# Polysketch attention and a multiplicative FFN: a planner with measured durations, key sums in four operations, filled waits and new ranks

## The chip, the cores and the metric

The kernel runs on one core of a Trainium2 chip. The metric is the device time of one execution in microseconds (us); lower is better. The profiled execution gives every instruction's start and duration on the core's engines: TensorE (PE, with its weight loads as PEld), VectorE (DVE), ScalarE (ACT), GpSimd (POOL) and SyncE (SP, which issues the DMAs).

## The reference

```python
def phi(x):                                   # S1, S2: 8 x 32; x: 4 x 4 x 1088 x 32
    a = np.einsum('rd,bhsd->bhsr', S1, x)
    b = np.einsum('rd,bhsd->bhsr', S2, x)
    return np.einsum('bhsi,bhsj->bhsij', a, b).reshape(*x.shape[:-1], r * r)
q_p, k_p = (phi(q), phi(k))
kv = np.einsum('bhsf,bhsd->bhfd', k_p, v)     # key sums
z = np.sum(k_p, axis=2)
num = np.einsum('bhsf,bhfd->bhsd', q_p, kv)
den = np.einsum('bhsf,bhf->bhs', q_p, z)[..., None] + 1e-06
x = (num / den).transpose(0, 2, 1, 3).reshape(4352, 128)
out = ((x @ w1) * (x @ w2) @ w3) @ w_out      # w1, w2: 128 x 1024; w3: 1024 x 1024; w_out: 1024 x 128
```

S1, S2 and the four FFN weights come in as float64 and reach the kernel as raw words; q, k and v are float32.

## The kernel before

**Key side, once for each of the 4 batches.** VectorE forms the maximum of the keys (`peak`), a rounded leading part and the remainder (`first`, `second`, `kk`). TensorE sums products over the keys into one PSUM tile, `ps_kvz`, in `products` (L688): `gs` is the Gram part from `kk`, `kv` the sum of key features `kp` times v. Each is a run of very small products, 32 columns wide: for a batch 64 products in each half of the Gram part (`gs0`, `gs1`), 24 for the 64 keys beyond 1024 (`rg`), 32 in each half of `kv` and 8 for the rest (`rv`). In TensorE's instructions each product is one product record and one weight load; the counts of a batch are 152 for `gs` and 72 for `kv`. The features `kp` come from the keys by head: `tr` (VectorE transposes, L618), `ab` (TensorE, L624), `ab_t` (L635), `kp` (L608). From the sums VectorE and TensorE then make the small matrices that the queries need: `fin1`, `T_mm`, `T_pair`, `N_mm`, `N_pair`, `kz` (L745 to L785).

**Query side, for 8 groups of 512 queries' positions in all heads and a rest (group 8).** Transposes (L1009), `grid`, `lead` (ScalarE), `rem`, then `ay` (TensorE), `split`, `dens`, `dens2` and `phi` (VectorE, L969, tile `ph`), `phT` (TensorE, L976, tile `ps_ph`), `pT` (ScalarE copy), `nd` (TensorE, L993, tile `ps_x`) and a ScalarE copy to `xT` (L1000), the FFN's input.

**FFN, for each group and 8 chunks of 128 hidden columns.** `a` (L1090) and `b` (L1100) on TensorE, the copy of `a` on ScalarE (L1095), `mul` on VectorE (L1105, tile `ab`), `o` (L1111, tile `ps_o`) on TensorE, and a transpose `oT` (VectorE, L1116) that is stored. w3 and w_out are folded into one matrix `w3o` (`ps_wt` L522, `ps_w3o` L534). The weights come in 22 chunks; ScalarE reads their words in three operations (L375, L378, L339) and VectorE makes float32 of them in two (`join` L387, `add` L390).

**The order.** The first 34 us are a list written by hand (L1165), with products of zeros (`idle`, L322) in TensorE's waits. All else is given as operations to a planner, `Plan` (L43 to L137): name, engine, duration, what is read and written, and a rank. It keeps a clock for each engine, and of the operations that can start within 0.1 us of the earliest it takes the one of lowest rank:

```python
t0 = min(c)[0] + 0.1
t, r, i = min((x for x in c if x[0] <= t0), key=lambda x: (x[1], x[2]))
```

PSUM has one bank each for `out`, `ps_kvz`, `t`, `wa` and `wb` and three (`h`) that `a` and `b` share. What the planner gives is issued in that order, and each engine keeps it (L1204 to L1211), so the planner's durations decide only the order; a wait on the chip is whatever the real durations make of it.

Of the kernel before, what the change touches and what calls it, by code (L numbers as in the profile page):

```python
# [37 lines left out]
COLUMNS = {"ay": 32, "ab": 32, "gs": 32, "kv": 32, "nd": 64}  # L38
TURN = 0.1
LATENCY = {"PE": 0.27, "DVE": 0.2, "ACT": 0.23, "POOL": 0.3, "SP": 2.5}  # L40


class Plan:  # L43
# [36 lines left out]
    def order(self):  # L80
# [3 lines left out]
        columns = 128  # L84
        turn = {}
# [14 lines left out]
        while left:  # L100
            best = {}
            for i in left:
# [38 lines left out]
def kernel(  # L141
# [178 lines left out]
    def idle(times, n=256):  # L320
        for _ in range(times):
            nc.tensor.matmul(idle_ps[:, :n], zeros[:, :128], zeros[:, :n], start=True, stop=True)  # L322
    idle(24)
    sgn = [consts.tile([128, CW], I32, tag=f"sgn{i}", name=f"sgn{i}") for i in range(2)]
# [190 lines left out]
    def weight_ops(first):  # L515
# [23 lines left out]
        for n in range(first, len(chunks)):  # L539
# [15 lines left out]
            for us, f in zip((0.62, 0.62, 0.7), words):  # L555
                p.op("words", "ACT", us, f, (("raw", n),), (("cv", n),), 0.3 if w_in else 3)
            for us, f in ((0.65, join), (0.62, add)):
                p.op("conv", "DVE", us, f, (("cv", n),), dst, 0.5 if w_in else 1.5)
            if name == "w3":
                ko, half = divmod(i, NH)  # L560
                p.op("w3_t", "PE", 0.44, lambda i=i: w3_t(i), dst, (("wa", "t", i),), 1)
                p.op("w3_t_copy", "ACT", 0.57, lambda i=i: w3_t_copy(i), (("wa", "t", i),), (("w3T", ko),), 1)
                if half == NH - 1:
                    p.op("w3_mm", "PE", 1.75, lambda ko=ko: w3_mm(ko), (("w3T", ko), *(("wo", x) for x in range(NC * DM // CW))),
                         (("wb", "mm", ko),), 1)
# [106 lines left out]
    def rest_ops(m, behind):  # L672
        nat, tr, tr_copy, ab, b_copy, feat = rest_steps(m)
        p.op("r_tr", "PE", 0.15, lambda: run_all((nat, tr)), (("k", 2 * m),), (("t", "r_tr"),), 0, (behind,))
        p.op("r_tr_copy", "ACT", 0.2, tr_copy, (("t", "r_tr"),), (("kT", "r"),), 0.5)
        p.op("r_ab", "PE", 0.22, ab, (("kT", "r"),), (("t", "r_ab"),))
# [3 lines left out]
    def k_steps(b):  # L680
# [561 lines left out]
```

## Time and profile before

| | us |
|---|---|
| runs: median (lowest to highest) of 3 | 305.8 (304.82 to 306.84) |
| profiled execution, its own time | 304.33 |
| its span, first to last instruction | 302.6 |
| TensorE busy | 279.8 |
| VectorE busy | 204.4 |
| ScalarE busy | 127.3 |
| mean granted TensorE clock | 0.989 |

The profiled execution is 1.5 us shorter than the median run, and 1.73 us of its time lie outside the span. Names in the profile's rows are those of tiles, an arrow from right to left reads "is made from", and the bracket at the end of a row is the idle time of that engine just before it with what ended it. A row of the timeline begins with its start in us.

### The profile page before, as it was taken

The page shows a single profiled execution, that of the slowest core. Times are in us where ns is not written, and L with a number is a line of the kernel's source. Part 1 is how long each engine was busy: PE and PEld are TensorE (multiplying, and loading weights), DVE is VectorE, ACT ScalarE, POOL GpSimd, SP SyncE. Part 2 cuts the span into 40 slices and gives each one's busy share as a digit, 9 for nine tenths or more (in the row PEclk, how much of TensorE's full clock was granted, in tenths as well). Part 3 has the DMA queues.
Part 4 walks back from the last instruction along what each step waited for, and adds up shares of the span by engine and source line. Part 5 has one row for each costly group of instructions (what it writes and reads, how often), then busy time and mean ns, then how long its engine had stood idle before and what let it go on. Part 6 is the DMA issues. An engine that isn't in the chain of part 4 may idle for free.

```text
span 302.6 us, 5558 instructions
## 1 busy us (share of the span) xinstructions
PE 279.8 (92%) x2214; PEld 159.7 (53%) x2214; DVE 204.4 (68%) x505; ACT 127.3 (42%) x244; POOL 7.1 (2%) x12
## 2 busy tenths in 40 slices
PE   7987889769999898959999999999999999999984
PEld 5866335336777556436644446454444453444653
DVE  6989799958999979994481279855845583642330
ACT  4634785839778591317302231224132333232111
POOL 0000000000000010000100001001000100000000
PEclk9999999979999999997999999999999999999999
DMA  5649995357781020000022010001100100200202
GB/s 156 215 100 310 254 319 229 89 192 208 221 202 69 0 76 2 3 1 0 2 35 35 0 27 12 2 1 18 19 0 5 31 0 0 35 2 1 35 2 50
DMA packets 28729, 22.37 MB, mean 74 GB/s; under 512 B 20000, under 2 KB 25248, under 8 KB 28704
## 3 DMA queue, kind: packets, MB, share of 16 engines
q1 hardware_dynamic: 28704, 22.03, 26.1%
q8 instruction: 17, 0.28, 0.4%
q14 instruction: 8, 0.07, 0.1%
HBM read 19.80 MB, written 2.23 MB: 73 GB/s over the span
## 4 chain that ended last, share of the span: by engine, by line
PE 74%; DVE 13%; DMA 6%; issue 3%; SPq 1%; ACT 1%; DVEq 0%; ACTq 0%
PE ps_o L1111 19%; PE b_ps L1100 18%; PE a_ps L1090 17%; PE ps_kvz L688 5%; DMA k_sb<-in_k_dram 5%; PE ps_w3o L534 4%; PE ps_x L993 2%; PE ps_wt L522 2%; PE ps_ph L976 2%; PE ps_c L894 2%; DVE ab L1105 2%; DMA qh<-in_q_dram 1%; DVE ph L969 1%; DVE kk L663 1%; PE ps_ab L624 1%
## 5 line engine op out<-in xcount | busy, mean ns | idle before, releaser
L1105 DVE TENSOR_TENSOR ab<-ffa,b_ps 128x512 f32<-128x512 f32 (+1 forms) x72 | 46.9, 653 | 61.6 <-PE b_ps L1100 60.7
L1095 ACT COPY ffa<-a_ps 128x512 f32<-128x512 f32 (+1 forms) x72 | 40.4, 561 | 109.7 <-PE a_ps L1090 109.0
L1090 PE MATMUL a_ps<-xT,w 128*128 128x512 f32 (+1 forms) x144 | 71.5, 578 | 1.7 <-ACT xT L1000 1.6
L1100 PE MATMUL b_ps<-xT,w 128*128 128x512 f32 (+1 forms) x144 | 71.6, 579 | 0.8 <-DVE ab L1105 0.5
L1111 PE MATMUL ps_o<-ab,w3o 128*128 128x512 f32 (+1 forms) x144 | 68.3, 577 | 0.8 <-DVE oT L1116 0.8
L1090 PEld LDWEIGHTS a_ps<-xT,w 128*128 128x128 f32 x144 | 26.6, 192 | 31.4 <-issue 20.5
L1100 PEld LDWEIGHTS b_ps<-xT,w 128*128 128x128 f32 x144 | 26.4, 192 | 30.3 <-issue 25.4
L1111 PEld LDWEIGHTS ps_o<-ab,w3o 128*128 128x128 f32 x144 | 25.7, 190 | 23.9 <-issue 19.6
L534 PEld LDWEIGHTS ps_w3o<-wo,w3T 128*128 128x128 f32 x128 | 15.4, 192 | 5.2 <-issue 4.1
L983 ACT COPY pT<-ps_ph 128x512 f32<-128x512 f32 (+1 forms) x18 | 9.4, 567 | 19.7 <-PE ps_ph L976 19.7
L339 ACT CAST sgn<-cv_c 128x512 f16<-128x512 f32 x22 | 16.9, 770 | 0.0
L534 PE MATMUL ps_w3o<-wo,w3T 128*128 128x128 f32 x128 | 15.8, 277 | 0.3 <-DVE bs L959 0.3
L375 ACT ACTIVATE cv_c<-raw 128x512 f32<-128x512 f32 x22 | 15.0, 682 | 0.8 <-DVE wo L387 0.8
L976 PE MATMUL ps_ph<-ident,ph 128*128 128x128 f32 x68 | 10.1, 290 | 5.4 <-DVE ph L969 5.3
L378 ACT ACTIVATE cv_m<-raw 128x512 int32<-128x512 uint32 x22 | 14.9, 676 | 0.3 <-DVE w3c L390 0.3
L322 PE MATMUL idle_ps<-zeros 128*128 128x256 bf16 x88 | 12.6, 308 | 1.7 <-DVE zeros L317 1.7
L976 PEld LDWEIGHTS ps_ph<-ident,ph 128*128 128x128 f32 x68 | 8.2, 147 | 10.1 <-issue 6.5
L387 DVE SCALAR_TENSOR_TENSOR w3c<-cv_c,sgn 128x512 int32<-128x512 int32 x16 | 10.8, 677 | 3.8 <-ACT sgn L339 3.8
L529 ACT COPY w3T<-ps_wt 128x512 f32<-128x512 f32 x16 | 9.3, 584 | 7.5 <-PE ps_wt L522 7.4
L993 PE MATMUL ps_x<-pT,kz 128*64 128x512 f32 (+1 forms) x48 | 10.8, 511 | 1.0 <-DVE k_ab L635 0.5
L322 PEld LDWEIGHTS <-zeros 128*128 128x128 bf16 x88 | 9.6, 112 | 3.8 <-DVE zeros L317 1.7
L867 POOL TENSOR_TENSOR q<-qT,q 128x512 f32<-128x512 f32 x5 | 5.8, 1154 | 230.5 <-ACT q L863 230.5
(180 smaller groups left out, 329.8 us busy)
## 6 DMA issues: line engine op xcount, KB each, us to landing
raw<-in_moe_w_dram SPq DMA_DIRECT2D x20, 512.0 KB, 5.7
qh<-in_q_dram SPq DMA_DIRECT2D x4, 544.0 KB, 6.7
k_sb<-in_k_dram SPq DMA_DIRECT2D x4, 512.0 KB, 5.2
out_dram<-oT SPq DMA_DIRECT2D x32, 64.0 KB, 1.9
kh<-in_k_dram SPq DMA_DIRECT2D x12, 128.0 KB, 5.8
v_sb<-in_v_dram SPq DMA_DIRECT2D x12, 128.0 KB, 4.4
raw<-in_moe_w_out_dram SPq DMA_DIRECT2D x2, 512.0 KB, 7.8
v_sb<-in_v_dram SPq DMA_DIRECT2D x1, 512.0 KB, 5.3
```

The source lines that it names most:

```text
L322: nc.tensor.matmul(idle_ps[:, :n], zeros[:, :128], zeros[:, :n], start=True, stop=True)
L339: nc.scalar.copy(bview(t.bitcast(F16)[:, 1:], [[2, n]]), c)
L375: nc.scalar.mul(x["c"], halves(raw[n], CW)[1].bitcast(F32), 2.0 ** -112)
L534: nc.tensor.matmul(ps["mm"], w3T[ko][:, c], wo[:, c], start=(c == 0), stop=(c == NC - 1))
L688: nc.tensor.matmul(out[h * D:(h + 1) * D], lhs, rhs, start=start, stop=stop, skip_group_check=True)
L976: nc.tensor.transpose(s["ps"][:, j * 128:(j + 1) * 128], s["ph"][:, j, 2 * p:2 * p + 2].rearrange("p h i j -> p (h i j)"), ident)
L993: nc.tensor.matmul(view(ps[64 * p:64 * (p + 1)]), kz_done[t if b is None else b][:, 64 * p:64 * (p + 1)], view(s["pT"][:, p, :n]), start=T ...
L1090: nc.tensor.matmul(a_sb[g, c, "ps"][:, :n], w1[:, c * 128:(c + 1) * 128], xT[key], start=True, stop=True)
L1095: nc.scalar.copy(a_sb[g, c][:, :n], a_sb.pop((g, c, "ps"))[:, :n])
L1100: nc.tensor.matmul(ab_sb[g, c, "ps"][:, :n], w2[:, c * 128:(c + 1) * 128], xT[key], start=True, stop=True)
L1105: nc.vector.tensor_mul(ab_sb[g, c][:, :n], a_sb.pop((g, c))[:, :n], ab_sb.pop((g, c, "ps"))[:, :n])
L1111: nc.tensor.matmul(o_ps[g][:, :n], w3o[:, c], ab_sb.pop((g, c))[:, :n], start=c == 0, stop=c == NC - 1)
```

## The change

The planner's durations are set to measured ones, most by a tenth of a microsecond or less. The key sums are four operations, `gs0`, `gs1` (with `rg`), `kv0` and `kv1` (with `rv`), each with its own place; before, they were two. A new rule counts TensorE's products: an operation is put off, in the plan's time, where more than 120 products (`MOST`) would have begun in the last 2 us (4 us in the first 60). `ps_kvz` is one tile for the whole kernel. Where TensorE waits over 0.6 us in the plan, products of zeros fill the wait; they go to columns of `ps_kvz` that nothing reads. The plan has two such places, 7 products ahead of `nd` of group 1 and 11 ahead of that group's first `a`. Ranks come from a table, `FIRST`: VectorE's key work goes from 1 to 2, `mul` from 0 to 0.55, and `o` is taken earlier (at 6 waiting chunks, was 8). Lines after the change are 21 to 26 higher.

TensorE around the end of batch 1's Gram sums (`ps_kvz`), before:

```order
L688 MATMUL ps_kvz<-kkr_218 32x64
L688 MATMUL ps_kvz<-kkr_218 32x32 x2
L522 MATMUL ps_wt<-ident,w3c 128x128 x4
L1100 MATMUL b_ps<-xT,w_71 128x512
L1090 MATMUL a_ps<-xT,w_70 128x512
L624 MATMUL ps_ab<-kT,S12blk 32x256 x8
L522 MATMUL ps_wt<-ident,w3c 128x128 x4
L1100 MATMUL b_ps<-xT,w_71 128x512
```

The same place after, at the end of the first half of these sums:

```order
L710 MATMUL ps_kvz<-kk 32x64
L710 MATMUL ps_kvz<-k_sb,kk 32x32
L1121 MATMUL b_ps<-xT,w_71 128x512
L544 MATMUL ps_wt<-ident,w3c 128x128 x4
L1111 MATMUL a_ps<-xT,w_70 128x512
L646 MATMUL ps_ab<-kT,S12blk 32x256 x8
L710 MATMUL ps_kvz<-kk 32x64
L710 MATMUL ps_kvz<-k_sb,kk 32x32
```

The 152 products of the Gram part stood in one run; now 64 are followed by five other operations and then 88. In batches 2 and 3 all 224 products stood in one run behind `ay`; now 64 stand alone, and 160 follow after `ab` and a `w3o` (batch 2) or after a `b` and an `a` (batch 3).

TensorE around the transposes `ps_ph` of the fourth query group, before:

```order
L443 MATMUL ps_N<-Ts,P_437 128x8
L1100 MATMUL b_ps<-xT,w_71 128x512
L1090 MATMUL a_ps<-xT,w_70 128x512
L1100 MATMUL b_ps<-xT,w_71 128x512
L781 MATMUL ps_kz<-ident,kvm 128x128
L976 MATMUL ps_ph<-ident,ph 128x128 x8
L522 MATMUL ps_wt<-ident,w3c 128x128 x4
L993 MATMUL ps_x<-pT,kz_1281 64x512 x2
L534 MATMUL ps_w3o<-wo,w3T 128x128 x8
```

and after:

```order
L556 MATMUL ps_w3o<-wo,w3T 128x128 x8
L1121 MATMUL b_ps<-xT,w_71 128x512
L1132 MATMUL ps_o<-ab,w3o 128x512
L1111 MATMUL a_ps<-xT,w_70 128x512
L997 MATMUL ps_ph<-ident,ph 128x128 x8
L1121 MATMUL b_ps<-xT,w_71 128x512
L544 MATMUL ps_wt<-ident,w3c 128x128 x4
L1014 MATMUL ps_x<-pT,kz_1269 64x512 x2
L544 MATMUL ps_wt<-ident,w3c 128x128 x4
L1111 MATMUL a_ps<-xT,w_70 128x512
L710 MATMUL ps_kvz<-kk 32x64
```

These transposes stood behind batch 2's sums and their `ps_T`, `ps_N` and `ps_kz`; now they and `ps_x` stand ahead of all of them.

VectorE at the `ph` that these transposes read, before:

```order
L776 TENSOR_TENSOR Rh<-Na,mask4n 128x32
L776 TENSOR_TENSOR Rf<-Na,mask_96 128x32
L776 TENSOR_TENSOR Rl<-Nb,mask_96 128x32
L1105 TENSOR_TENSOR ab<-ffa,b_ps 128x512 x2
L608 TENSOR_TENSOR kp<-k_ab 128x1024
L969 TENSOR_TENSOR ph<-ay,bs 128x1024
L390 ISA w3c<-w3c,cv_m 128x1024
```

and after:

```order
L975 TENSOR_REDUCE den<-pr 128x32
L977 SCALAR_TENSOR_TENSOR rc<-den 128x16
L978 RECIPROCAL rc<-rc 128x16
L980 TENSOR_TENSOR bs<-ay_C,rc 128x128
L990 TENSOR_TENSOR ph<-ay,bs 128x1024
L1126 TENSOR_TENSOR ab<-ffa,b_ps 128x512
L412 ISA w3c<-w3c,cv_m 128x1024
```

Between `bs` (the last step of the denominator) and `ph` stood `fin1`, `T_pair` and `N_pair` of batch 2, two `kp` of batch 3 and six `mul`; now nothing stands there.

TensorE's end, before:

```order
L1100 MATMUL b_ps<-xT,w_71 128x256
L1090 MATMUL a_ps<-xT,w_70 128x256
L1111 MATMUL ps_o<-ab,w3o 128x512
L1100 MATMUL b_ps<-xT,w_71 128x256
L1111 MATMUL ps_o<-ab,w3o 128x512
L1111 MATMUL ps_o<-ab,w3o 128x256 x8
```

and after:

```order
L1111 MATMUL a_ps<-xT,w_70 128x256
L1132 MATMUL ps_o<-ab,w3o 128x512
L1121 MATMUL b_ps<-xT,w_71 128x256
L1111 MATMUL a_ps<-xT,w_70 128x256
L1121 MATMUL b_ps<-xT,w_71 128x256
L1132 MATMUL ps_o<-ab,w3o 128x256 x8
```

The last `o` of group 7 (128x512) stood right ahead of the eight of the rest (128x256), which write the same bank; now three half products stand between. The diff, with the table of durations cut to a line or two:

```diff
-COLUMNS = {"ay": 32, "ab": 32, "gs": 32, "kv": 32, "nd": 64}
+COLUMNS = {"ay": 32, "ab": 32, "gs0": 32, "gs1": 32, "kv0": 32, "kv1": 32, "nd": 64}
+PRODUCTS = {"ay": 48, "ay2": 32, "ab": 16, "gs0": 64, "gs1": 88, "kv0": 32, "kv1": 40, "w3_mm": 16, "w3_t": 4}
+MOST = 120
+FIRST = {"words": 3, "conv": 1.5, "early": 1.5, "k": 2, "KX": 6, "q": 1, "q_act": 0.5, "k_act": 1, "a": 2, "b": 1.9, "o": 1.5,
+         "many": 6, "late": 3, "w3_t": 1, "w3_t_copy": 1, "w3_mm": 1, "k1": 1, "mul": 0.55}
...
+                if engine == "PE":
+                    room = MOST - PRODUCTS.get(ops[i][0], 2)
+                    for at, count in reversed(issued):
+                        room -= count
+                        if room < 0:
+                            t = max(t, at + (4.0 if at < 60 else 2.0))
+                            break
...
-    def idle(times, n=256):
+    kvz_ps = psum.tile([128, 512], F32, tag="kvz", name="ps_kvz")
+    late_ps = kvz_ps[:, 256:]
+    def idle(times, late=False):
         for _ in range(times):
-            nc.tensor.matmul(idle_ps[:, :n], zeros[:, :128], zeros[:, :n], start=True, stop=True)
+            nc.tensor.matmul(late_ps if late else idle_ps[:, :256], zeros[:, :128], zeros, start=not late, stop=True,
+                             skip_group_check=late)
     idle(24)
+    nc.tensor.matmul(late_ps, zeros[:, :128], zeros, start=True, stop=True)
...
-                ps = psum.tile([128, 128], F32, tag="kvz", name="ps_kvz")
+                ps = kvz_ps[:, :128]
...
-        op("first", "DVE", 1.25 if even else 1.0, (("k", b), ("gk", b)), (("kk", b),), rank)
+        op("first", "DVE", 1.63 if even else 1.25, (("k", b), ("gk", b)), (("kk", b),), rank)
...
-        p.op("gs", "PE", 2.2, lambda: run_all(st[x] for x in ("gs0", "gs1", "rg")), (("k", b), ("kk", b), ("kkr", m)),
+        p.op("gs0", "PE", 0.85, st["gs0"], (("k", b), ("kk", b)), (("kvz", b),))
+        p.op("gs1", "PE", 1.1, lambda: run_all(st[x] for x in ("gs1", "rg")), (("k", b), ("kk", b), ("kkr", m)), (("kvz", b),))
+        p.op("kv0", "PE", 0.6, st["kv0"], (("kp", b, 0), ("v", b)), (("kvz", b),))
+        p.op("kv1", "PE", 0.7, lambda: run_all(st[x] for x in ("kv1", "rv")), (("kp", b, 1), ("v", b), ("kpr", m)),
              (("kvz", b),))
-        p.op("kv", "PE", 1.35, lambda: run_all(st[x] for x in ("kv0", "kv1", "rv")),
-             (("kp", b, 0), ("kp", b, 1), ("v", b), ("kpr", m)), (("kvz", b),))
...
-                 lambda tiles, end: 1.5 if pend(tiles, end) > 8 else 3)
+                 lambda tiles, end: FIRST["o"] if pend(tiles, end) > FIRST["many"] else FIRST["late"])
...
+    busy = 0.0
     for t, n in p.order():
+        if p.ops[n][1] == "PE":
+            if t - busy > 0.6:
+                idle(int((t - busy - 0.3) / 0.107), late=True)
+            busy = t + p.ops[n][2]
         p.ops[n][3]()
```

More of the change, by code (lines that the diff above doesn't have):

```diff
@@ L1027, in op @@
             if rank is None:
-                rank = {"PE": 0, "DVE": 1, "ACT": 0.5, "POOL": 0}[engine]
+                rank = {"PE": 0, "DVE": FIRST["q"], "ACT": FIRST["q_act"], "POOL": 0}[engine]
             return p.op(f"{name}", engine, us, st[name], reads, writes, rank, after)
@@ L1034, in q_ops @@
         elif not skip:
[L1035 removed]
+            op("tr", "DVE", 0.75 if half else 0.62, (("qh", b),), (qT, ("qTr", b))[:1 + half], after=begin)
             if half and b + 2 < B:
                 p.op("load", "SP", 1.7, lambda: load_by_head("q", b + 2), (), (("qh", b + 2),))
[L1038 to L1039 removed]
+        op("grid", "DVE", 0.35 + 0.6 * w, (qT,), (("gq", g),), after=begin)
+        op("lead", "ACT", 0.2 + 1.2 * w, (qT, ("gq", g)), (("q1", g), ("q2", g)))
         op("rem", "DVE" if lean else "POOL", 0.62 if lean else 1.1, (qT, ("q1", g), ("q2", g)), (("q2", g),))
@@ L1176 @@
         for b in bs:
-            p.hold((which, b), 3.0 * (b - 1))
+            p.hold((which, b), 3.0 * (b - 1) + (2.4 if which == "qh" and b == 1 else 0))
     p.hold(("xT", 0), 0.3)
```

66 lines of the change are left out of this document (32 added, 34 removed).

## The prediction

> **What bounds the kernel now.** I read the page first: the busy line, then the slices for TensorE and its granted clock.
>
> ```profile
> PE 279.8 (92%) x2214; PEld 159.7 (53%) x2214; DVE 204.4 (68%) x505; ACT 127.3 (42%) x244; POOL 7.1 (2%) x12
> ...
> PE   7987889769999898959999999999999999999984
> PEclk9999999979999999997999999999999999999999
> ...
> q8 instruction: 17, 0.28, 0.4%
> ...
> PE 74%; DVE 13%; DMA 6%; issue 3%; SPq 1%; ACT 1%; DVEq 0%; ACTq 0%
> ```
>
> TensorE sets the time, with two slices in which its clock fell and holes around them; 3% of the chain is "issue", a wait that no other engine ends. The table by stretches (length; busy us of PE, PEld, DVE, ACT, POOL; granted clock; DMA share; GB/s) locates them:
>
> ```profile
> 34.10:61.10 27.00, 24.56 (x208) 11.81 (x208) 24.42 (x50) 21.56 (x37) 0.00 (x0) 1.00 0.68 222
> 61.10:68.20 7.10, 4.49 (x24) 2.38 (x22) 3.82 (x7) 2.69 (x5) 0.00 (x0) 0.76 0.52 182
> 68.20:132.40 64.20, 62.36 (x664) 41.16 (x663) 58.00 (x144) 40.27 (x74) 1.16 (x1) 1.00 0.33 92
> 132.40:142.10 9.70, 6.47 (x37) 4.68 (x37) 5.81 (x8) 4.53 (x9) 0.00 (x0) 0.82 0.00 0
> 142.10:260.10 118.00, 117.33 (x721) 56.98 (x719) 69.20 (x163) 34.24 (x61) 5.28 (x5) 1.00 0.08 14
> ```
>
> From 142 us TensorE is full (117.33 of 118.00), so what this change can win lies before that and in the tail. From 68 to 132 us VectorE too is busy, 58.00 of 64.20: there a gain of TensorE can be lost again. Three of TensorE's waits (total, times, longest):
>
> ```profile
> PE ps_kvz L688 <- issue: 4.2, 3, 2.6
> ...
> PE ps_x L993 <- DVE k_ab L635: 0.5, 1, 0.5
> ...
> PE ps_w3o L534 <- DVE bs L959: 0.3, 1, 0.3
> ```
>
> All three "issue" waits are in the key sums. Their rows in the timeline (start, us), with the starts of the first and the last batch's sums:
>
> ```profile
> 58.99 0.34 PE L688 MATMUL ps_kvz<-kk 128*32 128x64 f32 x8 [0.40 <-DVE kk L663]
> 63.74 0.57 PE L688 MATMUL ps_kvz<-kkr 64*32 64x32 f32 x14 [2.61 <-issue]
> 119.93 0.32 PE L688 MATMUL ps_kvz<-kp,v_sb 128*32 128x64 f32 x7 [0.95 <-issue]
> 185.28 0.32 PE L688 MATMUL ps_kvz<-kk 128*32 128x64 f32 x7
> 189.33 0.33 PE L688 MATMUL ps_kvz<-kp,v_sb 128*32 128x64 f32 x9 [0.67 <-issue]
> ```
> And the stretches that these stalls cut, in the columns of the table above:
>
> ```profile
> 0.00:61.20 61.20, 52.45 (x602) 33.69 (x602) 53.70 (x151) 37.20 (x78) 0.70 (x6) 1.00 0.69 210
> 61.20:119.50 58.30, 54.35 (x633) 37.28 (x633) 50.11 (x110) 39.35 (x73) 1.16 (x1) 0.97 0.42 122
> 119.50:189.20 69.70, 65.50 (x507) 35.24 (x508) 44.47 (x105) 20.17 (x36) 2.31 (x2) 0.98 0.07 12
> ```
>
> Between the stalls lie 633 + 633 = 1266 and 507 + 508 = 1015 recorded products and weight loads. With a few records missing these are 5 and 4 times 256, and 256 is what the instruction queue's 17 packets make of it: 2 x 2214 / 17 = 260. So I read the stalls as a late block of 256 instructions. From 185.28 to the stall's start (189.33 - 0.67) the sums take 3.38 us for 207 products (all but the last 17 of 224), 16.3 ns each with its weight load, so a block of sums alone is through in 128 x 16.3 ns = 2.1 us. The block after it arrived at most 4.75 us (63.74 - 58.99) and 4.05 us (189.33 - 185.28) after the sums began.
>
> **The change part by part.** The sum is made against the profiled execution's 304.33 us.
>
> *Key sums in four, spread: the stalls go, -4.2 us* (2.61 + 0.95 + 0.67). Batch 1 had 152 products in a row (304 instructions, over a block), batches 2 and 3 had 224; now 64, 88, 32 and 40 products stand apart in batch 1, 64 and then 160 in batches 2 and 3. Counting blocks along the new order and adding start-to-start durations of the old rows, the block with least time is in batch 3, 3.9 us with a `b` and an `a` in it, the next in batch 2, 4.5 us. Against "at most 4.05" the first may still stall 0.2 us. Bounds: 0 to -4.2; I take -4.2, since 3.9 is close to double the 2.1 that failed.
>
> *The half clock goes with its causes, -3.5 us.* Clock lost is (1 - 0.76) x 7.10 = 1.70 us after the 2.61 us stall, and (1 - 0.82) x 9.70 = 1.75 us after the hole in this row:
>
> ```profile
> 135.67 1.72 PE L976 MATMUL ps_ph<-ident,ph 128*128 128x128 f32 x8 [3.23 <-DVE ph L969]
> ```
> A wait of 1.50 us in the front left the clock at full:
>
> ```profile
> 30.25 1.39 PE L976 MATMUL ps_ph<-ident,ph 128*128 128x128 f32 x8 [1.50 <-DVE ph L969]
> ```
>
> The Trainium skill, "TensorE: Matmul & The Clock Gate", section "HAM oscillation — how this bites in real kernels", states as a rule that gaps up to about 3.4 us are harmless. Here the trace disagrees: 2.61 us was enough. By the rule the first 1.70 us would not be the gap's and would stay: 294.7 in place of 293, still in the forecast's range.
>
> *The fourth group's phi comes earlier, -2.2 us.* VectorE's rows:
>
> ```profile
> 36.19 0.71 DVE L1009 STREAM_TRANSPOSE qT<-qh 128x512 f32<-128x512 f32 x1 [1.86 <-DMA qh<-in_q_dram]
> 67.10 0.69 DVE L1105 TENSOR_TENSOR ab<-ffa,b_ps 128x512 f32<-128x512 f32 x1 [3.25 <-PE b_ps L1100]
> 122.89 0.68 DVE L1105 TENSOR_TENSOR ab<-ffa,b_ps 128x512 f32<-128x512 f32 x1
> 134.30 1.23 DVE L969 TENSOR_TENSOR ph<-ay,bs 128x1024 f32<-128x1024 f32 x1
> ```
>
> Between `bs` and `ph` stood 134.30 - 122.89 = 11.4 us of other work; now `ph` follows `bs` at once (what else changes sides comes to about nothing: `second`, a key transpose and `ab_t` go behind it; a conversion and two `mul` come ahead). VectorE's wait of 3.25 us is the stall and half clock of TensorE, and the 1.86 us for `qh` is filled, since a conversion and a `g_k` now stand ahead of that transpose. So `ph` starts at 134.30 - 11.4 - 3.25 - 1.86 = 117.8, and the transposes can run 135.67 - 134.30 = 1.4 later, at 119.2. TensorE came there at 135.67 - 3.23 = 132.4; it now comes 3.6 (two stalls), 1.7 (clock) and 1.3 (front, below) earlier, and 7.0 more for what is moved behind: 224 sums (3.65), two `a` and three `b` (5 x 0.86, price below), less about 0.9, by which the `w3o`, `o` and `wt` that come ahead outweigh T, N and `ab`, which go behind: 118.8. A wait of 0.4 is left of 3.23; as both walks are good to half a microsecond, I leave 1.0. Bounds: 0 gained if VectorE comes 2 us later, 3.23 if it comes 1 us earlier.
>
> *Front of group 1, -1.3 us.*
>
> ```profile
> 36.79 1.02 PE L1100 MATMUL b_ps<-xT,w 128*128 128x512 f32 x2
> 37.65 1.11 PE L1090 MATMUL a_ps<-xT,w 128*128 128x512 f32 x2
> 39.25 1.13 PE L1100 MATMUL b_ps<-xT,w 128*128 128x512 f32 x2 [0.50 <-DVE ab L1105]
> ...
> 42.18 1.13 PE L1090 MATMUL a_ps<-xT,w 128*128 128x512 f32 x2
> 43.60 1.10 PE L1100 MATMUL b_ps<-xT,w 128*128 128x512 f32 x2 [0.29 <-DVE w L390]
> ...
> 53.29 1.56 PE L993 MATMUL ps_x<-pT,kz 128*64 128x512 f32 x4 [0.24 <-ACT pT L983]
> 55.75 1.13 PE L1090 MATMUL a_ps<-xT,w 128*128 128x512 f32 x2 [0.90 <-ACT xT L1000]
> ```
>
> A product takes 37.65 - 36.79 = 0.86. Around the two waits the steps were 1.60 and 1.42, so 0.74 + 0.56 = 1.30 is lost. With VectorE's 1.86 us filled, its `mul` and conversion come in time and `phT` of group 1 too: the work ahead of it on VectorE shrinks by 1.86 and by one `g_q` of about a microsecond. Bounds: 0 to -1.3.
>
> *Fills, and a new wait, +0.2 us.* The fills are 7 products ahead of `nd` and 11 ahead of the first `a` of group 1, at 3.44 / 30 = 0.115 us each by
>
> ```profile
> 25.31 3.44 PE L322 MATMUL idle_ps<-zeros 128*128 128x256 bf16 x30
> ```
> which is 0.8 and 1.3 us against waits of 0.24 and 0.90 with about 0.25 of refilling each (0.74 - 0.50): a loss of up to 0.4; and nothing gained, since those waits halved no clock. I take +0.3. The first `wt` now stands three products behind group 1's first `a`; if its words are being converted then, it waits up to one conversion,
>
> ```profile
> L390 DVE CUSTOM_DVE_ANT_0 w3c<-w3c,cv_m 128x1024 uint16<-128x1024 uint16 x16 | 10.9, 684 | 0.3
> L387 DVE SCALAR_TENSOR_TENSOR w3c<-cv_c,sgn 128x512 int32<-128x512 int32 x16 | 10.8, 677 | 3.8 <-ACT sgn L339 3.8
> ```
> 1.4 us; queued behind it are `b`, `a` and the first sums. I take 0.7. The waits of 0.5 (`ps_x`) and 0.3 (`ps_w3o`) above go, as their VectorE steps come ahead: -0.8.
>
> *Tail, -1.4 us.*
>
> ```profile
> 266.87 0.63 PE L976 MATMUL ps_ph<-ident,ph 128*128 128x128 f32 x4 [0.57 <-DVE ph L969]
> 294.06 3.72 PE L1111 MATMUL ps_o<-ab,w3o 128*128 128x256 f32 x16 [0.81 <-DVE oT L1116]
> ```
> Three half products (3 x 0.43 = 1.3 us) now stand between the last `o` of group 7 and the first of group 8 and cover the 0.81; eight products in place of six stand ahead of the rest's `phT` and cover the 0.57. Neither adds work.
>
> Sum: -4.2 - 3.5 - 2.2 - 1.3 + 0.2 - 1.4 = -12.4, so 291.9 for a profiled execution; the median of the runs is 305.8 - 304.33 = 1.5 above it: **293**.
>
> **Rivals.** *(1) VectorE takes the front's gain back.* For it: 58.00 of 64.20 us busy, and `mul` no longer goes first on VectorE (rank 0.55, was 0). Then the fourth group's wait stays and, at 3.2 us, halves the clock again: 2.2 + 1.75 + some 1.5 of the front = 5.5, so 298.5. Against: the 11.4 us moved behind `ph`.
>
> *(2) The sums stall still.* 160 products (320 instructions) in a row are left in batches 2 and 3, more than the 152 that stalled for 2.61. Two stalls of 0.67 to 2.61 give 294.3 to 298.2, and with the clock halved after each, 301.7; about 297. Against: the block boundaries, as counted, fall inside.
>
> *(3) The stalls aren't the instruction's way in,* but come with the sums wherever they stand (all three are on `ps_kvz`). Then 4.2 + 1.70 stay: 299. Against: the distances of 5 and 4 times 256. The Trainium skill, "Runtime: NRT & Kernel Launch", section "Instruction fetch mechanics", says that crossing a block of 256 instructions costs little and is mostly hidden, which speaks for this one; no row of the trace shows a crossing that cost nothing next to such quick products.
>
> *(4) Slower.* `mul` ranked behind phi and ahead of the key work only: if it comes late after each `b`, TensorE finds no free bank for the next `a` or `b`, as in the 39.25 row. To end 1% above 305.8 this needs 308.9 - 293 = 15.9 us, 0.25 us on each of the 64 full products of `b`, half of the 0.50 of that row every time. Against: after 142 us, where most of them stand, VectorE is busy for 69.20 of 118.00, so a late `mul` finds it free.
>
> **How the numbers follow.** Forecast (289 to 296): 0.60. Rival 1: 0.18; 2: 0.09; 3: 0.07; 4: 0.03; better than 289: 0.03. The range takes in the forecast's cases and most of rivals 1 and 2 and the lower half of 3: 289 to 299. About 1% is what a measurement of this kernel tells from no change (302.7 to 308.9). Faster: 0.60 + 0.18 + 0.03 and most of 2 and 3, 0.92; the same 0.05, mostly parts of 1 to 3 together; slower 0.03.
>
> **What would show it.** In the profile of the changed kernel: no "issue" wait of `ps_kvz` above 0.2 us; no 7 in the clock's slices; `ps_ph` of the fourth group near 119 us with a wait under 1 us; the first `a` of group 1 near 54.4; no wait of the last `ps_o` for `oT`; a wait under 1.4 us at the first `ps_wt`. It is wrong if VectorE's wait only moves to another `ph`, or if "issue" stands in front of other rows.

## The result

The kernel after takes 291.35 us (290.13 to 292.7, median of 4 runs) against 305.63 us (304.82 to 306.84) before. The ratio is 0.953, with a 95% interval of 0.947 to 0.960. 293 us with a range of 289 to 299 had been forecast. The profiled execution took 290.24 us, its span is 288.4 us (302.6 before). Two of the four runs took 290.13 and 290.24 us at a mean granted clock of 0.996 to 0.998, two 292.46 and 292.7 at 0.988, so a difference of a microsecond or two between medians below can be the clock's.

The page of the kernel after: engines, TensorE and its granted clock in 40 slices, and the chain that ended last.

```profile
PE 277.6 (96%) x2233; PEld 160.2 (56%) x2233; DVE 204.3 (71%) x505; ACT 126.0 (44%) x244; POOL 7.7 (3%) x12
...
PE   7989699999999999999999999999999999999993
...
PEclk9999999999999999999999999999999999999999
...
q8 instruction: 17, 0.28, 0.4%
...
PE 89%; DVE 6%; ACT 3%; issue 1%; ACTq 0%; DVEq 0%
```

The holes and the two slices of lower clock are gone, and the chain goes through TensorE for 89% of the span, 74% before. The same 17 packets of instructions are loaded. Between the first `a` and the last `o` TensorE has one wait of a size left (total, times, longest):

```profile
PE a_ps L1111 <- ACT ffa L1116: 0.5, 1, 0.5
```

The work between four landmarks shows where the time went: the first `a` of group 0, the first `a` of group 1, the fourth group's `ps_ph`, and the last eight `o`. The table by stretches (length; busy us of PE, PEld, DVE, ACT, POOL; clock; DMA share; GB/s), first of before:

```profile
34.11:55.75 21.64, 19.61 (x65) 8.77 (x65) 19.20 (x41) 16.58 (x29) 0.00 (x0) 1.00 0.71 237
55.75:135.67 79.92, 71.84 (x830) 46.62 (x830) 70.22 (x163) 48.19 (x88) 1.16 (x1) 0.98 0.35 101
135.67:294.06 158.39, 156.35 (x910) 79.32 (x910) 85.79 (x202) 46.01 (x85) 5.28 (x5) 0.99 0.07 12
```

and of after:

```profile
34.29:55.72 21.43, 20.76 (x83) 10.29 (x83) 20.15 (x43) 16.23 (x29) 0.00 (x0) 1.00 0.72 241
55.72:117.75 62.03, 62.03 (x588) 41.14 (x589) 59.13 (x129) 47.60 (x89) 1.69 (x1) 1.00 0.44 129
117.75:280.05 162.30, 162.30 (x1151) 83.50 (x1150) 95.43 (x234) 45.52 (x84) 5.28 (x5) 1.00 0.07 12
```

The first stretch is 0.2 us shorter than before. The second is 17.9 us shorter, of which some 7 are work that moved into the third, longer by 3.9. Time in which TensorE does nothing falls from 2.03 + 8.08 + 2.04 = 12.15 us to 0.67, that is by 11.5; the clock gives back 1.70 + 1.75; the 18 fills take 2.3 us (their group's row stands below). That makes 12.6 of the 14.2 us by which the three stretches together are shorter. The rest, 1.6 us, is in no row; the point-by-point section returns to it.

### The profile page after: what moved, and what is told of

Its sections match the earlier page's. It is cut to its first block, busy times and chain, and to the rows that moved or that the text cites. A ratio compares the mean times of both kernels' runs of the same rounds, so it can differ in the third digit from the quotient of the medians.

```text
span 288.4 us, 5600 instructions
## 1 busy us (share of the span) xinstructions
PE 277.6 (96%) x2233; PEld 160.2 (56%) x2233; DVE 204.3 (71%) x505; ACT 126.0 (44%) x244; POOL 7.7 (3%) x12
## 4 chain that ended last, share of the span: by engine, by line
PE 89%; DVE 6%; ACT 3%; issue 1%; ACTq 0%; DVEq 0%
PE ps_o L1132 21%; PE a_ps L1111 20%; PE b_ps L1121 20%; PE ps_kvz L710 5%; PE ps_w3o L556 5%; PE ps_wt L544 3%; PE ps_x L1014 3%; PE ps_ph L997 2%; PE ps_c L915 2%; PE idle_ps L342 2%; PE ps_ab L646 1%; PE ps_ab L617 1%; PE ps_kvz L342 1%; PE ps_c L928 1%; ACT ffa L1116 1%
## 5 line engine op out<-in xcount | busy, mean ns | idle before, releaser
L1121 PE MATMUL b_ps<-xT,w 128*128 128x512 f32 (+1 forms) x144 | 70.7, 573 | 0.0
L342 PEld LDWEIGHTS <-zeros 128*128 128x128 bf16 x106 | 11.4, 110 | 4.8 <-DVE zeros L333 1.7
L1137 DVE STREAM_TRANSPOSE oT<-ps_o 128x512 f32<-128x512 f32 x8 | 5.7, 715 | 9.6 <-PE ps_o L1132 9.6
L412 DVE CUSTOM_DVE_ANT_0 w3c<-w3c,cv_m 128x1024 uint16<-128x1024 uint16 x16 | 11.0, 690 | 0.4
```

The lines of the kernel that those rows point to most:

```text
L342: nc.tensor.matmul(late_ps if late else idle_ps[:, :256], zeros[:, :128], zeros, start=not late, stop=True, skip_group_check=late)
L1121: nc.tensor.matmul(ab_sb[g, c, "ps"][:, :n], w2[:, c * 128:(c + 1) * 128], xT[key], start=True, stop=True)
```

## The experiments

Counts of products below are TensorE's, as in the prediction; a row of an order counts the code's products, of which a float32 product is two of these, a transpose (`ident`) or a product of zeros one.

### Where the instructions lie

The kernel before with 64 tiny products behind the first fills. All later instructions of TensorE stand 128 places on, half a block.

```diff
     idle(24)
+    for _ in range(64):
+        nc.tensor.matmul(idle_ps[:, :16], zeros[:, :128], zeros[:, :16], start=True, stop=True)
```

> The kernel before with one edit: 64 tiny products of zeros (16 columns) behind the first fills of TensorE, which moves every later instruction of TensorE by 128 places; nothing else moves. Theory A (a block of 256 instructions that comes too late): in batch 1 no block holds sums alone any more, so the 2.61 us stall and the half clock after it (1.7 us) go; in batches 2 and 3 a whole block of sums remains, so one stall of 0.7 to 1.4 us each remains, but 64 products earlier in the run: in the rest's Gram products (kkr), no longer among kp. In all 305.6 - 2.6 - 1.7 + 0.5, and 0 to 1.5 for the tiny products themselves: 302 to 303.5. Rival B (the sums stall wherever they stand, the place among the instructions does not matter): stalls of about 2.6, 0.95 and 0.67 at the same products as before, 305.6 to 307.

302.78 us against 306.16 (ratio 0.989, 0.977 to 1.000). The four runs go from 300.78 to 305.74, and the interval reaches 1.000, so the time alone does not tell this kernel from before. The rows do; they are from the longest of these runs, 305.74. Batch 1 has no "issue" wait; batches 2 and 3 have one each. The timeline of this kernel:

```profile
116.21 0.42 PE L690 MATMUL ps_kvz<-kkr 64*32 64x64 f32 x6 [1.28 <-issue]
187.91 0.43 PE L690 MATMUL ps_kvz<-kkr 64*32 64x32 f32 x8 [1.25 <-issue]
```

Both stand among the `kkr`, as theory A said, where before they stood among `kp`. So the sums do not stall of themselves: the place in the instruction stream decides where, and whether. Behind the first of the two the clock falls to half (table by stretches, columns as above):

```profile
118.11:121.52 3.41, 3.41 (x5) 1.38 (x5) 1.77 (x8) 0.59 (x1) 0.00 (x0) 0.50 0.00 0
```

The view of the DMA queues shows the load itself. In before, from 116 to 121 us, one packet of the instruction queue moves, in the eleventh of 40 slices (GB/s), at 117.3 us:

```profile
GB/s 0 0 0 0 0 0 0 0 0 0 131 0 0 0 0 0 0 0 0 0 0 0 0 0 0 0 0 0 0 0 0 0 0 0 0 0 0 0 0 0
...
q8 instruction: 1, 0.02, 1.6%
```

TensorE goes on at 119.93, 2.6 us later. (The packet itself takes 1.6% of 16 engines' 5 us, 1.3 us, so 1.4 us pass from its end.) In the shifted kernel, from 113 to 116 us, it is the eighth slice, 113.6 us, and TensorE goes on at 116.21, again 2.6 us later:

```profile
GB/s 0 0 0 0 0 0 0 218 0 0 0 0 0 0 0 0 0 0 0 0 0 0 0 0 0 0 0 0 0 0 0 0 0 0 0 0 0 0 0 0
...
q8 instruction: 1, 0.02, 2.8%
```

The kernel after, moved by 64 places in the same way:

```diff
     idle(24)
+    for _ in range(32):
+        nc.tensor.matmul(idle_ps[:, :16], zeros[:, :128], zeros[:, :16], start=True, stop=True)
```

> The kernel after with 32 tiny products of zeros behind the first fills, so that all later instructions of TensorE move by 64 places. By my count a block of 256 then lies wholly in batch 2's run of 160 products. Theory A: one issue wait of 0.7 to 1.4 us on the sums comes back, in batch 2, some 14 products before the end of the run, and none elsewhere; 291.4 + 1 = 292 to 293. Rival B (the run's length is what counts, 160 is short enough): no issue wait, 291.4 to 292.

294.27 us (ratio 0.964, 0.956 to 0.971), about 3 us slower than after, but not for the reason given. The forecast wait in batch 2 is not there as a wait; the sums slow down at the forecast place, by 0.3 us: 64 products take 132.62 - 131.28 = 1.34 us where 64 x 16.3 ns would be 1.04. It is one step among them, from 132.08 to 132.38, that takes 0.29 us, and it ends 2.6 us after a packet that starts at 129.73. The timeline:

```profile
131.28 1.42 PE L712 MATMUL ps_kvz<-kp,v_sb 128*32 128x64 f32 x64
132.62 0.32 PE L712 MATMUL ps_kvz<-kpr,vr 64*32 64x64 f32 x8
```

The shift also pushed a boundary into batch 0's sums, in the hand-written front, and there a stall came and half a clock with it. Its row in the timeline:

```profile
15.08 0.30 PE L712 MATMUL ps_kvz<-kkr 64*32 64x64 f32 x2 [1.13 <-issue]
```

And the stretch behind it in the table by stretches (columns as above), at a clock of 0.50:

```profile
17.33:24.16 6.83, 6.65 (x56) 4.84 (x44) 4.87 (x25) 1.00 (x3) 0.00 (x0) 0.50 0.40 91
```

So theory A holds in its place, but my size failed: a block of sums alone need not wait 0.7 us or more. In batch 2 of this kernel a `w3o` of 2.0 us stands right ahead of the 160 products; I take it that the load of the next block was asked for while TensorE was still busy with those longer products, whereas batch 1's sums in before had just waited for `kk` (0.40 in the prediction's row). That reading was not tried by itself.

### The sums joined again

The kernel after with two operations for the sums:

```diff
-MOST = 120
+MOST = 10 ** 6
...
-        p.op("gs0", "PE", 0.85, st["gs0"], (("k", b), ("kk", b)), (("kvz", b),))
-        p.op("gs1", "PE", 1.1, lambda: run_all(st[x] for x in ("gs1", "rg")), (("k", b), ("kk", b), ("kkr", m)), (("kvz", b),))
-        p.op("kv0", "PE", 0.6, st["kv0"], (("kp", b, 0), ("v", b)), (("kvz", b),))
-        p.op("kv1", "PE", 0.7, lambda: run_all(st[x] for x in ("kv1", "rv")), (("kp", b, 1), ("v", b), ("kpr", m)),
+        p.op("gs", "PE", 1.95, lambda: run_all(st[x] for x in ("gs0", "gs1", "rg")), (("k", b), ("kk", b), ("kkr", m)),
              (("kvz", b),))
+        p.op("kv", "PE", 1.3, lambda: run_all(st[x] for x in ("kv0", "kv1", "rv")),
+             (("kp", b, 0), ("kp", b, 1), ("v", b), ("kpr", m)), (("kvz", b),))
```

> The kernel after with the key sums as two operations again (gs 152 products, kv 72) and without the limit of 120; all other durations, ranks and fills stay. By my count of blocks, batch 1's run no longer fills a block alone, but in batches 2 and 3 all 224 products stand in a row and a whole block of 256 instructions lies in each. Theory A (late block): two issue waits on the sums, 0.7 to 1.4 us each, each ending 1.2 to 1.6 us after a packet of the instruction queue has landed; with up to one half-clock window (1.7 us) after each: 293 to 297. Rival B (the spreading gave nothing, the gain is the ranks' and durations'): no issue wait, 291.4.

291.24 us, and the kernel after, run beside it, 290.45:

> The kernel after, unchanged, as the measure for the three others and to see how the granted clock varies from run to run: spans of 288.4 with a clock of 0.996 to 0.998 and of 290.8 with 0.988 have been seen. If the clock makes the difference, each lower run is longer by what the clock lost; median 290 to 292.7.

(Ratios 0.950, 0.946 to 0.954, and 0.948, 0.943 to 0.952, which the intervals do not tell apart; the clock of this second series of after was 0.991 to 0.997, its spans 288.4 to 289.7.) The stalls come back, in all three batches, but small. The group of waits:

```profile
PE ps_kvz L710 <- issue: 1.3, 3, 0.7
```

The longest of them in the timeline:

```profile
178.47 0.64 PE L710 MATMUL ps_kvz<-kp,v_sb 128*32 128x64 f32 x29 [0.71 <-issue]
```

Their sum, 1.3 us, and at most some 0.8 us of time are what the four operations and the limit of 120 are worth in this order, not 4.2 and 1.7. Theory A is right that waits return, and this one ends in its 1.2 to 1.6 us after the packet has landed (last section); it had no wait in batch 1, where one of 0.42 us came, and its 293 to 297 us was missed. Rival B is nearly right on the time and wrong on the waits.

### The clock and the fills

The kernel before with 28 products of zeros in the 3.23 us wait ahead of the fourth group's `ps_ph`:

```diff
+    kvz_ps = psum.tile([128, 512], F32, tag="kvz", name="ps_kvz")
+    late_ps = kvz_ps[:, 256:]
+    nc.tensor.matmul(late_ps, zeros[:, :128], zeros, start=True, stop=True)
...
-                ps = psum.tile([128, 128], F32, tag="kvz", name="ps_kvz")
+                ps = kvz_ps[:, :128]
...
+    seen = 0
     for t, n in p.order():
+        if p.ops[n][0] == "phT0":
+            seen += 1
+            if seen == 3:
+                for _ in range(28):
+                    nc.tensor.matmul(late_ps, zeros[:, :128], zeros, start=False, stop=True, skip_group_check=True)
         p.ops[n][3]()
```

> The kernel before with 28 products of zeros (about 3.0 us) in the 3.23 us wait ahead of the fourth group's ps_ph; the wait itself stays. Theory (the idle window halves the clock, and fills count as work): the granted clock stays at 1.00 from 132 to 142 us and the rows ps_ph, ps_wt, ps_x take 0.87, 0.49 and 1.0 us from start to start in place of 1.54, 1.04 and 1.53; the time falls by 1.7 us, to 303.9. Rival (the clock falls for another reason, or products of zeros do not count): the same rows and 305.6. The three stalls stay in both.

304.75 us against 306.16 (ratio 0.996, 0.992 to 0.9995): a gain of 1.4, where 1.7 was forecast. The timeline behind the fills shows it directly:

```profile
137.98 1.07 PE L979 MATMUL ps_ph<-ident,ph 128*128 128x128 f32 x8 [0.17 <-DVE ph L972]
139.28 0.66 PE L525 MATMUL ps_wt<-ident,w3c 128*128 128x128 f32 x4 [0.24 <-ACT pT L986]
139.87 1.08 PE L996 MATMUL ps_x<-pT,kz 128*64 128x512 f32 x4
140.88 2.05 PE L537 MATMUL ps_w3o<-wo,w3T 128*128 128x128 f32 x16
```

`ps_ph` takes 1.07 us, 1.72 behind the unfilled wait (the prediction's row), and `ps_x` takes 140.88 - 139.87 = 1.01 where it took 139.78 - 138.25 = 1.53 in the timeline of the kernel before:

```profile
138.25 1.59 PE L993 MATMUL ps_x<-pT,kz 128*64 128x512 f32 x4
139.78 1.49 PE L534 MATMUL ps_w3o<-wo,w3T 128*128 128x128 f32 x11
```

The granted clock stays at 1.00 from 132 to 142 us, so products of zeros count as work, and the lower clock came from the wait. From `ps_ph` to `ps_w3o` it is 140.88 - 137.98 = 2.90 us here and 139.78 - 135.67 = 4.11 in before, 1.2 less: part of the 1.75 went into a new wait of 0.24 for `pT`.

The kernel after without its 18 fills, with 18 tiny products at the start so that the places behind the fills stay (those ahead of them, up to 52 us, move by 18 products):

```diff
     idle(24)
+    for _ in range(18):
+        nc.tensor.matmul(idle_ps[:, :16], zeros[:, :128], zeros[:, :16], start=True, stop=True)
...
             if t - busy > 0.6:
-                idle(int((t - busy - 0.3) / 0.107), late=True)
+                pass
```

> The kernel after without the 18 fills in the plan's waits; 18 tiny products at the start keep every later instruction in its place of 256. Theory (these fills hold nothing up but themselves): ps_x of group 1 starts 0.3 to 0.5 us sooner after ps_ph (1.73 us now), the first a of group 1 0.1 to 0.6 sooner than 55.72, the clock stays at 1.00 there; 290.8 to 291.3. Rival (the fills keep the clock up): a half clock for 3.4 us after 54 us, plus 1.7: 293.

292.79 us in 4 runs that spread from 290.69 to 295.34 (ratio 0.956, 0.947 to 0.965), so the time decides nothing. The timeline does, for the length of the chain (the kernel without fills):

```profile
51.97 1.04 PE L999 MATMUL ps_ph<-ident,ph 128*128 128x128 f32 x8
53.25 1.56 PE L1016 MATMUL ps_x<-pT,kz 128*64 128x512 f32 x4 [0.24 <-ACT pT L1006]
56.14 1.12 PE L1113 MATMUL a_ps<-xT,w 128*128 128x512 f32 x2 [1.33 <-ACT xT L1023]
```

From `ps_ph` to the first `a` it is 56.14 - 51.97 = 4.17 us without fills and 55.72 - 51.54 = 4.18 with them (rows below). They cost nothing. Ahead of them, the moved places brought a stall into batch 0's sums, in the hand-written front:

```profile
14.19 0.28 PE L712 MATMUL ps_kvz<-kkr 64*32 64x32 f32 x3 [0.49 <-issue]
```

The clock of the profiled execution stayed up without the fills; the other three runs had granted clocks of 0.974, 0.988 and 0.991, after's eight 0.988 to 0.998. As this stall too may have lowered the clock in those runs, what the fills do for the clock stays open.

### Ranks and durations

The kernel after with the ranks of before (`k` 1, `k_act` 0.5, `KX` 10, `mul` 0, `many` 8):

```diff
-FIRST = {"words": 3, "conv": 1.5, "early": 1.5, "k": 2, "KX": 6, "q": 1, "q_act": 0.5, "k_act": 1, "a": 2, "b": 1.9, "o": 1.5,
-         "many": 6, "late": 3, "w3_t": 1, "w3_t_copy": 1, "w3_mm": 1, "k1": 1, "mul": 0.55}
+FIRST = {"words": 3, "conv": 1.5, "early": 1.5, "k": 1, "KX": 10, "q": 1, "q_act": 0.5, "k_act": 0.5, "a": 2, "b": 1.9, "o": 1.5,
+         "many": 8, "late": 3, "w3_t": 1, "w3_t_copy": 1, "w3_mm": 1, "k1": 1, "mul": 0}
```

> The kernel after with the ranks of before (VectorE: key work 1, mul 0, KX 10; o from 8 waiting chunks), the rest as after, the fills by its own rule. Theory (the fourth group's phi is a matter of VectorE's ranks): its ph stands behind batch 2's fin1, T_pair, N_pair again, TensorE reaches ps_ph near 127 us and spends 2 to 3.2 us there, now on fills (its plan puts some there) and so at full clock; no issue wait; 293.5 to 295. Rival (the ranks do not matter, only durations and spreading): ps_ph near 118 without a wait, 291.4.

299.21 us (ratio 0.979, 0.972 to 0.985): 8.8 us over after, more than forecast. The fourth group's `ps_ph` is back behind `ps_kz`, and the planner, which saw the wait coming, filled it (timeline):

```profile
132.34 0.27 PE L803 MATMUL ps_kz<-ident,kvm 128*128 128x128 f32 x1
132.45 2.78 PE L342 MATMUL ps_kvz<-zeros 128*128 128x256 bf16 x24
135.07 1.04 PE L997 MATMUL ps_ph<-ident,ph 128*128 128x128 f32 x8
```

Two single ranks. `mul` at 0, as before:

```diff
-         "many": 6, "late": 3, "w3_t": 1, "w3_t_copy": 1, "w3_mm": 1, "k1": 1, "mul": 0.55}
+         "many": 6, "late": 3, "w3_t": 1, "w3_t_copy": 1, "w3_mm": 1, "k1": 1, "mul": 0}
```

> The kernel after with only the rank of mul back at 0 (0.55); fills by its own rule (18 again). Its order still has the fourth group's ps_ph ahead of batch 2's T, N and kz. Theory (it is the key work's rank that moves phi, mul's place costs little): ps_ph of the fourth group with a wait under 1 us, waits and fills after 35 us together as in after (about 3.7 us), 290 to 292. Rival (mul's rank carries the gain): 295 to 299, as with all old ranks.

291.2 us (ratio 0.952, 0.948 to 0.956), 0.75 above the second series of after, which the intervals do not tell apart. And the key work alone:

```diff
-FIRST = {"words": 3, "conv": 1.5, "early": 1.5, "k": 2, "KX": 6, "q": 1, "q_act": 0.5, "k_act": 1, "a": 2, "b": 1.9, "o": 1.5,
+FIRST = {"words": 3, "conv": 1.5, "early": 1.5, "k": 1, "KX": 6, "q": 1, "q_act": 0.5, "k_act": 1, "a": 2, "b": 1.9, "o": 1.5,
```

> The kernel after with only VectorE's key work back at rank 1 (2); mul, KX and the rest as after; fills by its own rule (some 65, so the plan sees long waits). Theory (key work ahead of phi on VectorE makes TensorE wait): the fourth group's ps_ph comes behind 130 us, waits and fills together 9 to 12 us after 35 us, the clock stays at 1.00, 296 to 300. Rival: 291 to 292.

296.73 us (ratio 0.971, 0.967 to 0.974). The group of late fills (count, busy us, mean ns) in after:

```profile
L342 PE MATMUL ps_kvz<-zeros 128*128 128x256 bf16 x18 | 2.3, 273 | 0.0
```

With `k` 1:

```profile
L342 PE MATMUL ps_kvz<-zeros 128*128 128x256 bf16 x65 | 8.6, 273 | 0.0
```

And with all the old ranks:

```profile
L342 PE MATMUL ps_kvz<-zeros 128*128 128x256 bf16 x61 | 7.6, 273 | 0.0
```

With `k` 1 there are 47 fills more, 6.3 us, and the time is 6.3 us longer: what looks like busy TensorE is a wait that was planned. (That TensorE would have waited as long without them was not tried. With all the old ranks TensorE's `ps_ph` at 135.07 begins 0.17 us after VectorE's `ph` ends at 134.90, so the 24 fills cover a real wait; with `k` 1 some may run longer than they need.) The place differed from my forecast, though. The fourth group's `ps_ph` came at 125.56, not behind 130, and the fills stood at several places.

So of the ranks it is the key work's that carries most of the gain, 6.3 of 8.8 us (`many`, `KX` and `k_act` were not tried alone). I read it as keeping work of VectorE that nobody waits for yet behind work that TensorE waits for; no single wait stands for it.

The durations of before in the planner, and with them the time at which it lets the queries of batch 1 (`qh`) arrive, 2.4 us earlier than in after; all else as after. Of the changed lines three:

```diff
-        op("first", "DVE", 1.63 if even else 1.25, (("k", b), ("gk", b)), (("kk", b),), rank)
+        op("first", "DVE", 1.25 if even else 1.0, (("k", b), ("gk", b)), (("kk", b),), rank)
...
-        op("split", "DVE", 0.85 + 1.3 * w, (A,), (("hl", g),))
+        op("split", "DVE", 0.6 + 1.35 * w, (A,), (("hl", g),))
...
-        op("dens2", "DVE", 0.5 + 0.66 * w, (("pr", g), B_), (("bs", g),))
+        op("dens2", "DVE", 0.4 + 0.65 * w, (("pr", g), B_), (("bs", g),))
```

> The kernel after with the planner's durations of before (and the hold of qh), the new ranks, the spreading and the fills by its own rule. Theory (durations only shuffle the order): the fourth group's ps_ph still comes ahead of batch 2's sums, near 118 to 120 us; blocks with sums take 2.9 us in batches 2 and 3 by my count, so an issue wait of 0 to 0.6 us in each; 291.4 to 293.5. Rival (measured durations carry the gain): new waits of TensorE on VectorE of over 2 us in all, 294 to 297.

294.81 us (ratio 0.961, 0.956 to 0.966), 4.4 above after, more than theory and within the rival's 294 to 297. The fourth `ps_ph` came at 117.50, as the theory had it; but VectorE was late in other places, where after waits 0.49 at most. How much of this is the durations' and how much the arrival's was not separated. Its groups of waits, of which 1.5 for `ph` is the front's, in after too:

```profile
PE ps_ph L997 <- DVE ph L990: 2.1, 2, 1.5
...
PE b_ps L1121 <- DVE ab L1126: 1.4, 1, 1.4
PE ps_kvz L710 <- DVE kk L685: 0.9, 2, 0.5
```

### The front, tried further

In after the first `a` of group 1 begins at 55.72, as before. TensorE's timeline of after:

```profile
51.54 1.04 PE L997 MATMUL ps_ph<-ident,ph 128*128 128x128 f32 x8
...
53.27 1.10 PE L1014 MATMUL ps_x<-pT,kz 128*64 128x512 f32 x4
...
55.72 1.12 PE L1111 MATMUL a_ps<-xT,w 128*128 128x512 f32 x2
```

And ScalarE's:

```profile
52.17 1.07 ACT L1004 COPY pT<-ps_ph 128x512 f32<-128x512 f32 x2 [0.71 <-PE ps_ph L997]
53.13 0.73 ACT L883 ACTIVATE q<-qT,g_q 128x512 f32<-128x512 f32 x1
53.90 0.72 ACT L884 ACTIVATE q<-q,g_q 128x512 bf16<-128x512 f32 x1
54.53 0.67 ACT L397 ACTIVATE cv_c<-raw 128x512 f32<-128x512 f32 x1
55.09 0.57 ACT L1021 COPY xT<-ps_x 128x512 f32<-128x512 f32 x1
```

Between `pT` and `xT` ScalarE now does the two steps of group 2's `lead` and a conversion. I moved `lead` behind the copy to `xT`, and the `rem` that follows from it behind the next `first`; the fills ahead of `a` are cut to 64 columns each:

```diff
+        if late and times == 11:
+            for _ in range(times):
+                nc.tensor.matmul(kvz_ps[:, 256:320], zeros[:, :128], zeros[:, :64], start=False, stop=True, skip_group_check=True)
+            return
...
+    after_this = {"lead": ("nd_copy", 1), "rem": ("first", 1)}
...
+        name = p.ops[n][0]
+        count[name] = count.get(name, 0) + 1
+        if name in after_this and count[name] == 2:
+            held[name] = p.ops[n][3]
+            continue
         p.ops[n][3]()
+        for x, (behind_op, nth) in after_this.items():
+            if x in held and behind_op == name and count[name] == nth:
+                held.pop(x)()
```

> The kernel after with ScalarE's lead of group 2 moved behind the copy to xT of group 1 (and VectorE's rem of group 2, which waits for it, behind first), and the 11 fills ahead of the first a of group 1 cut to 64 columns, so that no place of 256 moves. Theory (the front's gain was lost to ScalarE's lead between pT and xT): the copy to xT starts 0.6 to 0.7 us sooner, the first a of group 1 at about 55.0 in place of 55.7; 0.4 to 0.7 us off the time: 289.8 to 290.8. Rival (the chain through pT, ps_x and xT takes as long anyway): a at 55.7, 290.5 to 291.4.

290.87 us (ratio 0.953, 0.949 to 0.956), no better than after. The step itself did what it should, the copy at 54.37 and `a` at 55.00; and then the wait that the prediction had put at the first `ps_wt` was there (timeline):

```profile
55.00 1.12 PE L1114 MATMUL a_ps<-xT,w 128*128 128x512 f32 x2 [0.26 <-ACT xT L1024]
...
59.15 0.63 PE L547 MATMUL ps_wt<-ident,w3c 128*128 128x128 f32 x4 [1.30 <-DVE w3c L415]
```

The 0.7 us won at `a` is lost at `ps_wt`, which waits for nothing in after's timeline,

```profile
58.49 0.63 PE L544 MATMUL ps_wt<-ident,w3c 128*128 128x128 f32 x4
```

and begins there 0.66 us sooner: the conversions, pushed back by `lead`, end the front. The same with 12 more products of zeros in the front's 1.51 us wait:

```diff
-             k0["N_pair"], *of(q0, "ay1 rem"), v0, v1, q0["ay2"], q1["tr"], lambda: load_by_head("q", 2), pause(30),
+             k0["N_pair"], *of(q0, "ay1 rem"), v0, v1, q0["ay2"], q1["tr"], lambda: load_by_head("q", 2), pause(42),
```

> As the run with xT first, and 12 more products of zeros in the 1.51 us wait of the hand-written front ahead of the first ps_ph. Theory (in some runs this wait and the two behind it make a window that halves the clock): the granted clock is 0.994 or more in all runs, and the median is that of the best runs, 289.4 to 290.2. Rival (the clock's lower runs come from elsewhere): runs with a clock of 0.988 to 0.991 as before, no gain over the run with xT first.

291.14 us (ratio 0.952, 0.950 to 0.955) and clocks of 0.996 to 1.000 in five runs; without them, 0.988 in one of six and 0.996 or more in the others. One low run in six against none in five does not show that the longer fill keeps the clock up, and the time is no better. No variant here is shown to beat after.

## Why the prediction was right, point by point

The total was right: 293 forecast, 291.35 measured, and for the profiled execution 291.9 against 290.24. Three of its six terms had the right size. Of the other three, the front gained 1.3 less than forecast, and the fourth phi and the fills 1.0 more each; that these nearly cancel is luck.

- **Stalls, -4.2.** No issue wait is left in after, and 3.9 us in a block, by my count, was enough, with no trace of the 0.2 us I had left open. The mechanism is shown: a shift alone removes batch 1's stall and moves the others, and the waits end a nearly fixed time after a packet of instructions. Why batch 1's packet started so late stays open (last section). But the step credited the four operations. Joined again in the new order they bring back 1.3 of the 4.2 us; the rest went with the new order, and whether by the longer products ahead of the sums or by the other boundaries was not tried.
- **Clock, -3.45.** 0.998 in after; filling the one wait alone gave 1.4 of 1.75; the 1.70 behind batch 1's stall was not tried by itself. The Trainium skill, "TensorE: Matmul & The Clock Gate", section "HAM oscillation — how this bites in real kernels", gives as its rule no idle gaps above about 3.4 us. In the shifted kernel after, a 1.13 us wait among the batch 0 sums was followed by 6.8 us of half clock, so the trace disagrees still more than it did in the prediction.
- **The fourth phi, -2.2.** It was mis-sized: the whole 3.23 went. TensorE came at 117.75 (118.8 forecast), and `ph` ended in time since VectorE began it at 116.11, where 117.8 had been worked out (why it was 1.7 us sooner still was not looked into). VectorE's row in the timeline:

```profile
116.11 1.22 DVE L990 TENSOR_TENSOR ph<-ay,bs 128x1024 f32<-128x1024 f32 x1
```

- **Front, -1.3.** This step failed: the first `a` of group 1 came 0.03 us sooner, at 55.72, where 54.4 had been named. TensorE reached `ps_ph` only 0.39 us sooner (51.54 for 51.93), an `a` ahead of it now waits 0.49 for ScalarE, and ScalarE's `lead` took the rest between `pT` and `xT`. I had walked VectorE and TensorE and left out ScalarE, which is busy for 16.58 of these 21.64 us in before. The size also depends on the execution: from the first `a` of group 0 to that of group 1 before took 21.64 us, but the same front took 22.32 in the trace of before shifted and 22.49 with fills, and the executions of after 21.43 and 21.42.
- **Fills and the new wait, +0.2.** No wait at `ps_wt` and no cost of the fills: -0.8 in place of +0.2. The wait exists as soon as `a` comes earlier, as the run with `xT` first shows.
- **Tail, -1.4.** Both waits are gone. The rest's `ps_ph` and the last `o` stand in the timeline without a wait:

```profile
257.30 0.60 PE L997 MATMUL ps_ph<-ident,ph 128*128 128x128 f32 x4
280.05 3.62 PE L1132 MATMUL ps_o<-ab,w3o 128*128 128x256 f32 x16
```

With the sizes that came out, the terms make -4.2 - 3.45 - 3.2 - 0.0 - 0.8 - 1.4 = -13.1 of the 304.33 - 290.24 = 14.1 us. The sum left out the refilling behind each wait, 0.25 us, which I had worked out in the front and did not count for the three stalls and the fourth `ps_ph`: 4 x 0.25 = 1.0 us has the size of what is missing. That is an estimate from two rows of the front; the four shorter waits that went as well would by the same reckoning add as much again, so it does not settle where the last microsecond is. Of the rivals, the first did not come (VectorE is busy 59.13 of 62.03 us in the second stretch and still not late), the second did not come in after but came in part when the places moved, and the third is refuted by the shift. The rule of the Trainium skill named beside the third ("Runtime: NRT & Kernel Launch", section "Instruction fetch mechanics": a crossing is mostly hidden) holds for after, where none of 17 packets is waited for; in before three were, for 4.2 us in all. Of the fourth rival, `mul` at rank 0 is no better than at 0.55.

## What to carry to other kernels

An "issue" wait inside a run of very small instructions points to the loading of the code: count instructions between such waits in blocks, and look for the packet of the instruction queue that lands just before each ends; a shift by half a block tells whether it is so, at the price of one line. When a planner moves work, walk every engine on the chain, the lightly used one too: a gain on one of them is passed on only as far as the next queue lets it. A planner's fills turn waits into busy time, so compare waits and fills together. A product added anywhere moves all places behind it: look for new waits in every later run of small instructions.

## What the runs showed of the hardware

A wait on the code ends 2.4 to 2.6 us after its packet starts in the three cases shown, in before, in before shifted and with the sums joined again. Of the 13 "issue" waits in the traces of all runs, twelve end 2.2 to 2.7 us after the start of the packet before them and one 3.2; counted from the packet's end, all 13 end 1.2 to 1.6 us after it. The third of the cases shown is seen here, with the packet in the second of 40 slices from 176 to 179 us (176.1), and TensorE going on at 178.47:

```profile
GB/s 0 218 0 0 0 0 0 0 0 0 0 0 0 0 0 0 0 0 0 0 0 0 0 0 0 0 0 0 0 0 0 0 0 0 0 0 0 0 0 0
```

What sets the start of a packet is open. In batches 2 and 3 of before it starts 1.7 and 1.8 us ahead of TensorE's stop (117.28 and 118.98, 186.86 and 188.66); in batch 1, the longest wait, it starts at 61.41, after TensorE had stopped at 61.13. The queues were moving much data then (a DMA share of 0.52 from 61 to 68 us in the prediction's table), but no run takes that traffic away.

Whether a wait halves the clock is not a matter of its length alone. 1.13 us and 1.28 us in the middle of small sums were followed by half a clock in the shifted kernels; 1.51 us between full-width products of zeros and `ps_ph` was not, in any profile here. The half clock does not last equally long either: 6.83 us behind batch 1's wait of 2.7 us in the kernel before with fills, 3.4 behind the 2.61 us in before. What else decides (when the wait falls, or how little work the sums are) was not separated.
